# A linear recurrence and its feed-forward block: feed-forward and exclusive decay sum in whole 128x128 tiles, and a new fixed order of steps

## The chip, the cores and the metric

One core of a Trainium2 chip runs the whole kernel. Its engines work in parallel and meet at semaphores: TensorE (matrix products and transposes, results in PSUM), VectorE, ScalarE, GpSimd, and SyncE, which issues most DMAs. The metric is the device time of one execution in microseconds (us); less is better. In the profile's rows PE is TensorE's matrix products, PEld its loads of the stationary operand, DVE is VectorE, ACT ScalarE, POOL GpSimd, SP SyncE.

## The reference

Batch 4, 8 heads, 768 time steps, head size 40; float32 in and out. First a recurrence over time, with a 40x40 state for each of the 32 pairs of batch and head:

```python
for t in range(S):
    y[:, :, t] = np.einsum('bhd,bhde->bhe', rt, state)
    Sa = np.einsum('bhde,bhe->bhd', state, at)
    state_decay = state * wt[:, :, None, :] - np.einsum('bhd,bhe->bhde', Sa, bt)
    state = state_decay + np.einsum('bhd,bhe->bhde', vt, kt)
```

Then y, as 3072 tokens of 320 features (8 heads times 40), goes through a feed-forward block of width 2048:

```python
h = x @ w_in
r = np.maximum(h, 0.0)
g = r * r
return g @ w_out
```

## The kernel before

**Tiling.** Time is cut into 12 chunks of 64 steps (`NCH`, `L`). Within a chunk the recurrence becomes matrix products: cumulative sums of log-decays, scaled copies of k, b, a, r, masked 64x64 triangles, and a state that passes from chunk to chunk. Since a head has 40 features and a chunk 64 steps, nearly all products use half of TensorE's 128x128 array: either two halves of its rows (`64*128` in the rows of the profile: 64 rows, 128 columns) or two halves of its columns (`128*64`). Two such products, one for each half, run at the same time. The kernel calls the two forms "R" and "C" in the third argument of `pe`.

**Steps.** `load`, `prep`, `rec`, `read` and `ffn` make one set of named steps for each chunk; `weights` makes those that load the two matrices. Those that matter here:

- `ld..`: loads of w, k, b, a, v, r, by SyncE (lines 372 to 398), into two buffers each.
- `ln`, `hi`, `lo` (lines 409 to 417): logarithm of the decay, split into two bfloat16 parts.
- `ci`, `cx`, `cg` (lines 430 to 456): inclusive, exclusive and whole sums of the log-decay. `cx` has 8 products of 320 columns, in column halves, against the triangle `UTX` (a 64x64 triangle in each of two diagonal corners of a 128x128 matrix that is zero elsewhere).
- `TK`, `TA`, `TV`, `TS`, `XT`: transposes. `EN`, `CX`: the triangles. `AS`, `EV`, `NU`, `S`, `SC`, `RS`, `Y`: products of the recurrence. Each has a step in small letters that moves its result out of PSUM (`tK`, `mEN`, `u0`, `s` and so on).
- `y` (line 702): VectorE multiplies the result of `Y` by a decay factor and writes it to `Yb`; `yd` (line 708) copies the 640 values once more beside it, so that both halves of the array find them; `XT` (line 721) transposes them in 20 pieces; `xt` moves 1280 columns out of PSUM.
- `F` (line 742): for each chunk four groups u0 to u3 of 20 products of 256 columns, in row halves: 320 features are five blocks of 64, and the two row halves hold the same features of x and different columns of `w_in`. `f`: maximum with zero, by ScalarE or VectorE. `q`: square, by GpSimd or VectorE.
- `O` (line 769): four groups of 16 products of 320 columns, in column halves. `o` moves the result, `st` stores it.

**Order.** Nothing is scheduled by a compiler. The string `ORDER` lists all steps in the order of issue, each with its engine; for TensorE's steps the digit is one of four PSUM slots (`pb0` to `pb3`). Every engine runs its steps strictly in this order, and waits where an operand is not there or a buffer is still in use. Durations that the program gives to `plan.add` (`LAT`, `SWITCH`, `FETCH`, the 2000 of a load) served to make this string and do nothing on the chip. All matrix products are recorded with line 356, all transposes with line 360, since helpers `mm` and `tp` emit them.

Of the kernel before, what the change touches and what calls it, by code (L numbers as in the profile page):

```python
# [7 lines left out]
FP32 = mybir.dt.float32  # L8
BF16 = mybir.dt.bfloat16
# [14 lines left out]
class Plan:  # L24
# [6 lines left out]
    LINE, FETCH = 256, 3500  # L31
# [51 lines left out]
ORDER = """SP ldw 0; SP ldk 0; SP ldw 1; SP ldr 0; ACT ln 0; POOL hi 0; SP ldb 0; POOL zu 2; DVE lo 0; SP lda  # L83
0; PE0 ci 0 h0; PE1 ci 0 h1; POOL zu 1; ACT ei 0 h0; PE2 cx 0; PE cg 0; SP ldr 1; ACT ex 0; ACT ei
0 h1; SP ldw 2; ACT ln 1; ACT eg 0; POOL hi 1; SP ldv 0; DVE mulKB 0 h1; POOL castR 0; DVE mulKB 0
h0; POOL lo 1; PE3 TK 0; SP lda 1; DVE mulA 0; ACT tK 0; POOL zu 0; PE0 ci 1 h0; PE1 TA 0; SP ldk
1; PE2 cx 1; ACT tR 0 g1; DVE tA 0; POOL castR 1; ACT ei 1 h0; DVE tR 0 g0; PE3 EN 0 g1; PE cg 1;
ACT ln 2; DVE mEN 0 g1; SP ldb 1; PE0 EN 0 g0; PE1 ci 1 h1; ACT ex 1; POOL hi 2; DVE mEN 0 g0; ACT
eg 1; ACT castV 0; POOL lo 2; SP ldb 2; ACT ei 1 h1; PE3 EV 0; DVE mulA 1; ACT u0 0 g1; PE2 cx 2;
SP ldv 1; ACT u0 0 g0; PE0 TA 1; ACT tR 1 g1; PE NU 0; PE cg 2; ACT u1 0 g1; DVE u1 0 g0; SP lda  # L90
2; ACT ex 2; DVE tA 1; PE1 S 0; ACT eg 2; POOL mulKB 1 h1; PE3 ci 2 h1; DVE mulKB 1 h0; ACT tR 1
g0; PE2 ci 2 h0; DVE s 0 q0; SP ldk 2; POOL win3; ACT ei 2 h1; PE0 TK 1; DVE s 0 q1; PE3 TV 0; DVE
tK 1; SP ldr 2; ACT tV 0; PE1 EN 1 g0; PE0 EN 1 g1; DVE mEN 1 g0; POOL castV 1; ACT ei 2 h0; PE3
AS 1; DVE mEN 1 g1; PE1 TS 0; PE2 CX 0 g1; ACT tS 0; POOL win1; DVE mCX 0 g1; PE EV 1; SP ldv 2;
PE0 CX 0 g0; ACT u0 1 g1; DVE mCX 0 g0; ACT u0 1 g0; POOL mulKB 2 h1; PE NU 1; DVE mulKB 2 h0; PE1
Y 0; ACT u1 1 g0; PE2 TK 2; DVE y 0; ACT u1 1 g1; SP ldw 3; DVE mulA 2; ACT tK 2; PE0 TV 1; POOL
castR 2; PE1 S 1; DVE yd 0; POOL win0; PE SC 1; DVE tV 1; SP lda 3; PE3 XT 0; PE2 TA 2; ACT xt 0;
DVE s 1 q1; PE0 CX 1 g0; ACT tR 2 g1; DVE s 1 q0; PE3 F 0 u3; ACT tA 2; DVE mCX 1 g0; PE1 TS 1;
POOL castV 2; ACT tR 2 g0; DVE tS 1; PE0 CX 1 g1; ACT f 0 u3; PE2 F 0 u1; SP ldw 4; DVE mCX 1 g1;
ACT ln 3; PE1 EN 2 g0; PE3 EN 2 g1; ACT f 0 u1; POOL hi 3; DVE mEN 2 g0; PE0 RS 1; PE Y 1; SP ldb  # L100
3; POOL lo 3; PE2 AS 2; DVE mEN 2 g1; PE1 F 0 u0; DVE y 1; POOL win2; SP ldk 3; PE EV 2; ACT f 0
u0; PE3 cx 3; DVE yd 1; DVE u0 2 g1; PE0 ci 3 h1; ACT u0 2 g0; PE cg 3; POOL q 0 u1; ACT ei 3 h1;
PE NU 2; ACT eg 3; PE1 ci 3 h0; DVE u1 2 g0; ACT u1 2 g1; PE0 XT 1; ACT ln 4; DVE xt 1; PE2 S 2;
POOL q 0 u0; PE SC 2; ACT ei 3 h0; SP ldr 3; PE0 TV 2; DVE s 2 q0; ACT ex 3; PE1 F 1 u1; DVE tV 2;
POOL wout0; PE3 F 1 u3; ACT f 1 u1; DVE s 2 q1; PE0 F 1 u0; POOL hi 4; ACT f 1 u3; DVE mulA 3;
POOL wout1; PE1 F 0 u2; DVE lo 4; ACT f 1 u0; DVE mulKB 3 h0; PE2 CX 2 g0; POOL mulKB 3 h1; PE3 CX
2 g1; ACT f 0 u2; PE0 F 1 u2; DVE mCX 2 g1; PE1 cx 4; ACT f 1 u2; POOL castR 3; DVE mCX 2 g0; PE
cg 4; POOL wout2; SP ldr 5; PE3 TK 3; ACT ex 4; PE0 ci 4 h0; POOL q 0 u2; DVE tK 3; PE2 TA 3; ACT
eg 4; PE1 RS 2; ACT tR 3 g0; PE Y 2; DVE tA 3; SP ldv 3; ACT tR 3 g1; PE3 O 0 u0; POOL wout3; ACT
ei 4 h0; DVE y 2; SP ldw 5; PE2 EN 3 g0; DVE yd 2; PE O 0 u1; DVE mEN 3 g0; PE0 EN 3 g1; POOL q 1  # L110
u0; PE1 ci 4 h1; DVE mEN 3 g1; PE2 XT 2; ACT ei 4 h1; PE O 0 u2; DVE q 1 u1; POOL q 0 u3; PE1 AS
3; PE0 O 1 u0; SP ldk 4; DVE zu 3; ACT castV 3; DVE q 1 u2; PE O 1 u1; DVE q 1 u3; ACT xt 2; SP
ldb 4; PE EV 3; PE O 1 u2; DVE u0 3 g1; ACT u0 3 g0; PE O 0 u3; PE NU 3; DVE o 0; ACT ln 5; PE O 1
u3; ACT u1 3 g1; DVE u1 3 g0; POOL hi 5; SP st 0; PE2 TS 2; SP lda 4; ACT o 1; POOL zu 4; DVE lo
5; PE3 TV 3; ACT tS 2; PE1 F 2 u1; SP ldr 4; DVE tV 3; POOL castR 5; PE0 F 2 u0; ACT f 2 u1; DVE
mulKB 4 h0; PE2 CX 3 g0; SP ldk 5; PE3 F 2 u3; ACT f 2 u0; POOL q 2 u1; DVE mCX 3 g0; SP lda 5;
PE1 CX 3 g1; PE0 ci 5 h0; ACT f 2 u3; DVE mulKB 4 h1; PE2 F 2 u2; POOL q 2 u0; DVE mCX 3 g1; ACT
ei 5 h0; SP ldb 5; PE3 cx 5; ACT f 2 u2; PE0 RS 3; DVE q 2 u3; PE cg 5; POOL castR 4; PE Y 3; ACT
ex 5; DVE mulA 4; PE1 ci 5 h1; POOL q 2 u2; SP ldv 4; PE2 TK 4; ACT eg 5; DVE y 3; ACT ei 5 h1;
PE3 TA 4; PE1 S 3; DVE tK 4; ACT tA 4; PE SC 3; POOL yd 3; SP ldw 6; PE0 O 2 u0; ACT tR 4 g0; DVE  # L120
s 3 q0; POOL mulA 5; ACT tR 4 g1; PE2 EN 4 g1; PE O 2 u1; DVE mEN 4 g1; SP ldr 6; PE3 XT 3; DVE s
3 q1; POOL mulKB 5 h0; PE2 EN 4 g0; ACT xt 3; PE O 2 u2; DVE mulKB 5 h1; SP st 1; DVE mEN 4 g0;
# [719 lines left out]
```

## Time and profile before

| | us |
|---|---|
| median of 3 runs | 269.33 |
| lowest and highest | 268.33, 271.39 |
| the profiled execution | 270.12 |
| its span, first to last instruction | 268.4 |

The span leaves out what lies around the program, so it is a little less than the time of the same execution. TensorE's granted clock was 0.975 of full speed on average; it was at half speed from 46.7 to 53.5, from 63.8 to 67.2 and from 128.6 to 132.1 us.

| stage of the recurrence or the block, by the groups of the profile | busy us, mean ns of one |
|---|---|
| F, 960 products in row halves | 60.8, 273 |
| O, 768 products in column halves | 59.4, 300 |
| q on GpSimd, 30 | 57.6, 1929 |
| q on VectorE, 18 | 17.5, 979 |
| f on ScalarE, 48 | 49.0, 1024 |

A product's own duration contains its way through the array; products that follow one another overlap, so what one costs is the distance between starts, not its duration. "Idle before" and "waits" say how long an engine stood still and what released it; "issue" there means that the profile names no releaser.

DMA engines were 62.8% busy with SyncE's queue, in packets under 512 bytes for the most part, and nearly all loads are done by 201 us: 165 GB/s in the slice of the span before, 8 GB/s in the one after.

### The profile page before, as it was taken

What the parts mean: (1) busy time and instruction counts of PE and PEld (TensorE: products, weight loads), DVE (VectorE), ACT (ScalarE), POOL (GpSimd) and SP (SyncE); (2) the same over time, 40 slices, a digit from 0 to 9 for tenths busy, and PEclk for the clock granted to TensorE, in tenths of its full rate; (3) what the DMA queues carried; (4) which work ended last, traced back from release to release, by engine and by line L of the source; (5) the groups of instructions that cost most, each with busy time, mean ns of one, the idle gap of its engine ahead of it and who ended that gap; (6) DMA issues with size and microseconds to landing.
All of it is one profiled execution on the core that took longest, in us unless ns stands there. A gap on an engine that the chain in (4) does not pass through costs nothing.

```text
span 268.4 us, 14323 instructions
## 1 busy us (share of the span) xinstructions
PE 226.9 (85%) x6712; PEld 193.6 (72%) x6712; DVE 198.1 (74%) x219; ACT 160.1 (60%) x201; POOL 141.5 (53%) x119
## 2 busy tenths in 40 slices
PE   0557884987979998997998898997879999999992
PEld 0335774776869986876888786886767888878881
DVE  7456578495886797996789898894888697867620
ACT  3346565636735774674674784775756877674631
POOL 4384634086570686674599287793483293232020
PEclk9999999597999999999799999999999999999999
DMA  7999999975993579799898298799980410200213
GB/s 116 185 185 143 153 193 149 136 127 58 171 171 56 114 142 142 180 169 153 181 155 116 53 145 155 133 124 171 158 165 8 89 19 2 54 5 2 51 26 74
DMA packets 135995, 31.06 MB, mean 116 GB/s; under 512 B 125185, under 2 KB 135937, under 8 KB 135937
## 3 DMA queue, kind: packets, MB, share of 16 engines
q1 hardware_dynamic: 131136, 27.53, 62.8%
q0 software_dynamic: 4800, 2.62, 7.7%
q8 instruction: 52, 0.85, 1.4%
q14 instruction: 7, 0.05, 0.1%
HBM read 28.84 MB, written 3.93 MB: 122 GB/s over the span
## 4 chain that ended last, share of the span: by engine, by line
PE 63%; DVE 13%; issue 7%; ACT 5%; DMA 5%; SPq 4%; POOL 3%; ACTq 0%; POOLq 0%; DVEq 0%
PE pb L356 55%; PE pb L360 8%; DMA raw_kb<-in_k_dram 2%; DVE KB L352 2%; DMA raw_r<-in_r_dram 2%; POOL lo L350 1%; ACT VU L342 1%; DVE EN L542 1%; DVE Yb L337 1%; DVE VU L339 1%; SPq L385 1%; SPq L778 1%; POOL tR L346 1%; DVE Yb L702 1%; ACT VUT L342 1%
## 5 line engine op out<-in xcount | busy, mean ns | idle before, releaser
L755 POOL TENSOR_TENSOR G<-G 128x1024 bf16<-128x1024 bf16 x30 | 57.6, 1929 | 53.0 <-ACT G L747 52.6
L356 PE MATMUL pb<-WOUT,G 128*64 128x320 bf16 x768 | 59.4, 300 | 3.8 <-issue 3.7
L747 ACT ACTIVATE G<-pb 128x1024 bf16<-128x1024 f32 x48 | 49.0, 1024 | 22.2 <-PE pb L356 21.1
L356 PE MATMUL pb<-XT,WIN 64*128 64x256 bf16 x960 | 60.8, 273 | 1.0 <-issue 0.9
L356 PEld LDWEIGHTS <-WIN 64*128 64x128 bf16 x960 | 46.9, 96 | 6.4 <-issue 1.7
L356 PEld LDWEIGHTS <-G 128*64 128x64 bf16 x768 | 42.9, 110 | 11.4 <-issue 5.5
L542 DVE TENSOR_TENSOR EN<-pb,MSK 128x1024 bf16<-128x1024 f32 x24 | 29.1, 1221 | 6.3 <-PE pb L356 6.0
L542 DVE TENSOR_TENSOR CX<-pb,MSK 128x1024 bf16<-128x1024 f32 x24 | 29.0, 1218 | 4.4 <-PE pb L356 4.2
L346 POOL CAST hi<-lnW 128x640 bf16<-128x640 f32 x11 | 8.6, 779 | 37.1 <-ACT lnW L409 17.9
L431 ACT ACTIVATE iG<-pb 128x640 f32<-128x640 f32 x24 | 16.8, 702 | 11.3 <-PE pb L356 10.6
L352 DVE TENSOR_TENSOR KB<-raw_kb,iG 128x640 bf16<-128x640 f32 x17 | 18.8, 1113 | 6.2 <-ACT iG L431 3.7
L356 PEld LDWEIGHTS <-EN 128*64 128x64 bf16 x768 | 16.4, 118 | 7.4 <-issue 5.3
L342 ACT ACTIVATE NZ<-pb 64x640 bf16<-64x640 f32 x19 | 13.2, 697 | 13.6 <-PE pb L356 9.0
L634 DVE TENSOR_TENSOR STb<-pb,gL 64x640 bf16<-64x640 f32 x22 | 18.1, 821 | 4.2 <-PE pb L356 3.7
L342 ACT ACTIVATE AR<-pb 128x512 bf16<-128x512 bf16 (+1 forms) x24 | 15.5, 667 | 8.3 <-PE pb L360 5.4
L753 DVE TENSOR_TENSOR G<-G 128x1024 bf16<-128x1024 bf16 x18 | 17.5, 979 | 3.0 <-ACT G L747 3.0
L342 ACT ACTIVATE VU<-pb 64x640 bf16<-64x640 f32 x15 | 10.5, 698 | 9.8 <-PE pb L356 7.3
L339 DVE TENSOR_SCALAR VU<-pb 64x640 bf16<-64x640 f32 x9 | 7.4, 823 | 10.0 <-ACT VU L342 6.2
L350 POOL TENSOR_TENSOR KB<-raw_kb,iG 128x640 bf16<-128x640 f32 x7 | 11.4, 1628 | 5.8 <-DMA raw_kb<-in_k_dram 3.6
L356 PE MATMUL pb<-hi,UTI 64*128 64x320 bf16 x48 | 8.6, 342 | 7.0 <-POOL hi L346 6.9
L342 ACT ACTIVATE osb<-pb 128x640 f32<-128x640 f32 x11 | 7.8, 705 | 11.2 <-PE pb L356 11.1
L350 POOL TENSOR_TENSOR lo<-lnW,hi 128x640 bf16<-128x640 f32 x8 | 13.0, 1622 | 2.4 <-PE pb L360 2.0
(88 smaller groups left out, 454.3 us busy)
## 6 DMA issues: line engine op xcount, KB each, us to landing
raw_w<-in_w_dram SPq DMA_DIRECT2D x24, 160.0 KB, 5.0
raw_kb<-in_k_dram SPq DMA_DIRECT2D x12, 320.0 KB, 6.1
raw_r<-in_r_dram SPq DMA_DIRECT2D x24, 160.0 KB, 4.1
raw_kb<-in_b_dram SPq DMA_DIRECT2D x12, 320.0 KB, 6.7
raw_a<-in_a_dram SPq DMA_DIRECT2D x24, 160.0 KB, 5.2
raw_v<-in_v_dram SPq DMA_DIRECT2D x12, 320.0 KB, 6.6
out_dram<-osb SPq DMA_DIRECT2D x24, 160.0 KB, 2.7
WIN<-in_moe_w_in_dram POOLq DMA_DIRECT2D x8, 160.0 KB, 4.6
```

The costliest lines, as they stand in the source:

```text
L342: alts.append(("ACT", c_act(n), lambda: nc.scalar.activation(out=o_(), in_=i_(), func=ACTF.Copy, scale=1.0 if scale is None else scale)))
L346: lambda: nc.gpsimd.tensor_copy(out=o_(), in_=i_())))
L350: return [("POOL", 130 + 2.35 * n, lambda: nc.gpsimd.tensor_tensor(out=o_(), in0=a_(), in1=b_(), op=op)), ("DVE", c_dve(n), lambda: nc.vec ...
L352: ("DVE", c_dve(n), lambda: nc.vector.tensor_tensor(out=o_(), in0=a_(), in1=b_(), op=op))]
L356: return lambda: nc.tensor.matmul(out=o_(), lhsT=l_(), rhs=r_(), start=start, stop=stop, skip_group_check=True)
L360: return lambda: nc.tensor.transpose(out=o_(), in_=i_(), identity=IDb[rows(g), :])
L431: ew(f"ei {c} h{jh}", [("ACT", c_act(2 * n), lambda hb=hb, jh=jh: nc.scalar.activation(out=iG[0][:].rearrange("p (g j) e -> p g (j e)", g= ...
L542: evac(f"m{nm} {c} g{g}", lambda s, n: [("DVE", c_dve(n), lambda: nc.vector.tensor_tensor(out=dst[q2][:, g, s].rearrange("p q i t -> p (q ...
L634: ew(f"s {c} q{q}", [("DVE", c_dve(2 * n), lambda q=q: nc.vector.tensor_tensor(out=STb[q2][rows(q), :, q, 0:D], in0=slot(hs, FP32)[rows(q) ...
L747: ("ACT", c_act(1024), lambda gb=gb, hf=hf: nc.scalar.activation(out=gb, in_=slot(hf, FP32)[:], func=ACTF.Relu)),
L753: ("DVE", 165 + 0.7 * 1024, lambda gv=gv: nc.vector.tensor_tensor(out=gv, in0=gv, in1=gv, op=ALU.mult)),
L755: ("POOL", 1900, lambda gv=gv: nc.gpsimd.tensor_tensor(out=gv, in0=gv, in1=gv, op=ALU.mult))],
```

## The change

Five edits, and a new `ORDER`. In the third argument of `pe` a form "D" is added for products that use the whole array.

1. `F` has 8 products with 128 rows and 128 columns of the array (two blocks of 128 features, for four groups of 128 columns of `w_in`) instead of 20 halves. A new step `FL` adds the last 64 features in 4 row halves. `f` now follows `FL`. PSUM slot and size of the result are as before.
2. `O` has 8 whole products instead of 16 halves.
3. `cx` has 4 whole products instead of 8 halves.
4. `Yb` holds 320 features and then the last 64 once more; `yd` writes these 64 by the same multiplication from PSUM (128 values in a partition) instead of copying 640; it runs on VectorE only. `XT` has 12 transposes instead of 20, and `xt` moves 768 columns instead of 1280.
5. `WIN` holds 256 features in two blocks of 128, by four DMAs; `WLAST` the last 64 by two DMAs in a new step `wlast`. They were eight DMAs.

In `pe` the durations that served to make the order are restated, and in `load` those of the loads. TensorE's matrix products and transposes go from 6712 to 5800 in all. In the order, `f` is on ScalarE 45 times and on VectorE 3 (48 and 0 before), `q` on GpSimd 37 times and on VectorE 11 (30 and 18); many other moves out of PSUM change between VectorE and ScalarE.

```diff
-    def pe(name, mode, cols, mms, tiles=2, **kw):
+    def pe(name, mode, cols, mms, **kw):
...
-        for jh in range(2):
-            for x in (h_, l_):
-                for g in range(2):
-                    ms.append(mm(
-                        lambda g=g, jh=jh: slot(hx, FP32)[rows(g), jh, 0:n].rearrange(
-                            "p (j e) -> p j e", e=D),
-                        lambda g=g: UTX[:, rows(g)],
...
-        pe(f"cx {c}", "C", n, ms, reads=[("hi",), ("lo",)], writes=[hx], alloc=[hx])
+        for x in (h_, l_):
+            for jh in range(2):
+                ms.append(mm(
+                    lambda jh=jh: slot(hx, FP32)[:, jh, 0:n].rearrange("p (j e) -> p j e", e=D),
+                    lambda: UTX[:],
...
+        pe(f"cx {c}", "D", n, ms, reads=[("hi",), ("lo",)], writes=[hx], alloc=[hx])
...
-        ew(f"yd {c}", copy_alts(lambda: Yb[q2][:, :, :, 1, :], lambda: Yb[q2][:, :, :, 0, :], 640,
-                               True, engines=("DVE", "POOL")),
-           reads=[("Yb", q2, 0)], writes=[("Yb", q2, 1)])
+        def out_y(f0, f1, to):
+            return [("DVE", c_dve(2 * (f1 - f0)), lambda: nc.vector.tensor_tensor(
+                out=Yb[q2][:, :, to:to + f1 - f0], in0=slot(hy, FP32)[:, :, f0:f1],
+                in1=Gex[c % NG][:].rearrange("p (s j) e -> p s (j e)", s=2)[:, :, f0:f1],
+                op=ALU.mult))]
...
+        ew(f"yd {c}", out_y(n - 64, n, n), reads=[hy, ("Gex", c % NG)], writes=[("Yb", q2, 1)],
+           free=[hy])
...
-        for kb_ in range(NKB):
+        for k3 in range(3):
...
-            for i in range(2):
-                for kb_ in range(NKB):
-                    for rg in range(2):
...
-                            lambda rg=rg, kb_=kb_, i=i, u=u: WIN[
-                                rows(rg), kb_, 256 * u + 128 * i:256 * u + 128 * i + 128],
-                            lambda rg=rg, kb_=kb_: XT[q2][rows(rg), kb_, :],
...
-            pe(f"F {c} u{u}", "R", NT, ms, reads=[("XT", q2), ("WIN", u)], writes=[hf],
+            for rg in range(2):
+                for i in range(2):
+                    for k2 in range(2):
...
+                            lambda rg=rg, k2=k2, i=i, u=u: WIN[
+                                :, k2, 512 * u + 256 * rg + 128 * i:
+                                512 * u + 256 * rg + 128 * i + 128],
+                            lambda k2=k2: XT[q2][:, k2, :], i == 0 and k2 == 0, False))
+            pe(f"F {c} u{u}", "D", NT, ms, reads=[("XT", q2), ("WIN", u)], writes=[hf],
                alloc=[hf])
+            ms = []
+            for i in range(2):
+                for rg in range(2):
+                    ms.append(mm(
+                        lambda rg=rg, i=i, hf=hf: slot(hf, FP32)[:, rg, NT * i:NT * i + NT],
+                        lambda rg=rg, i=i, u=u: WLAST[
+                            rows(rg), u, 128 * i:128 * i + 128],
+                        lambda rg=rg: XT[q2][rows(rg), 2, :], False, True))
+            pe(f"FL {c} u{u}", "R", NT, ms, reads=[("XT", q2), ("WLAST",)], writes=[hf])
...
-                    for bb in range(2):
-                        ms.append(mm(
-                            lambda g=g, bb=bb: slot(ho, FP32)[rows(bb), g, 0:DM],
-                            lambda g=g, bb=bb, j=j: G[q2][
-                                :, j, (2 * g + bb) * L:(2 * g + bb) * L + L],
-                            lambda j=j: WOUT[:, j, :], j == 0, j == NFB - 1))
+                    ms.append(mm(
+                        lambda g=g: slot(ho, FP32)[:, g, 0:DM],
+                        lambda g=g, j=j: G[q2][:, j, 2 * g * L:2 * g * L + 2 * L],
+                        lambda j=j: WOUT[:, j, :], j == 0, j == NFB - 1))
```

The beginning of the order, before and after (the whole string has 911 steps before and 960 after):

```diff
-ORDER = """SP ldw 0; SP ldk 0; SP ldw 1; SP ldr 0; ACT ln 0; POOL hi 0; SP ldb 0; POOL zu 2; DVE lo 0; SP lda
-0; PE0 ci 0 h0; PE1 ci 0 h1; POOL zu 1; ACT ei 0 h0; PE2 cx 0; PE cg 0; SP ldr 1; ACT ex 0; ACT ei
+ORDER = """SP ldw 1; SP ldw 0; SP ldr 0; SP lda 0; SP ldb 0; ACT ln 0; SP ldk 0; POOL hi 0; POOL castR 0; DVE
+lo 0; ACT ln 1; PE0 ci 0 h0; SP ldr 2; PE1 cx 0; PE2 ci 0 h1; PE cg 0; ACT ei 0 h1; POOL hi 1; ACT
```

A later place of the new order, where `F` and its `FL` have other steps between them:

```diff
+DVE q 1 u2; PE3 cx 4; ACT o 0; DVE f 2 u3; PE1 F 2 u0; PE2 F 2 u1; SP ldr 4; PE FL 2 u0; POOL
+castV 3; PE0 TS 2; ACT f 2 u0; PE FL 2 u1; DVE tS 2; PE cg 4; PE1 AS 3; ACT ex 4; POOL q 1 u3; SP
```

On TensorE, 808 products and transposes stand ahead of the first `F` in the order before, 952 in the new one.

## The prediction

> **What bounds the kernel now.** I read the page first (busy shares, chain of waits, DMA queues), then TensorE's waits, its timeline, and the windows by stage.
>
> ```profile
> PE 226.9 (85%) x6712; PEld 193.6 (72%) x6712; DVE 198.1 (74%) x219; ACT 160.1 (60%) x201; POOL 141.5 (53%) x119
> PE 63%; DVE 13%; issue 7%; ACT 5%; DMA 5%; SPq 4%; POOL 3%; ACTq 0%; POOLq 0%; DVEq 0%
> q8 instruction: 52, 0.85, 1.4%
> ```
>
> TensorE is the bound, and it executes nearly all of the program: 6712 matmuls and 6712 weight loads of 14323 instructions. The chain has 7% "issue", time in which TensorE waited for nothing that the profile names. The last line offers a cause: 0.85 MB of instructions in 52 packets is 16 KB a packet, and 13424 TensorE instructions over 52 is 258 a packet.
>
> ```profile
> PE pb L356 <- issue: 11.4, 11, 2.9
> PE pb L360 <- issue: 1.3, 2, 0.7
> ```
>
> Thirteen unnamed waits, 12.7 us. The timeline shows where they fall:
>
> ```profile
> 186.95 0.41 PE L360 MATMUL pb<-IDb,Yb 64*128 64x64 bf16 x15 [0.51 <-issue]
> 187.17 0.65 PE L360 MATMUL pb<-IDb,STb 64*128 64x64 bf16 x32
> 187.64 0.65 PE L360 MATMUL pb<-IDb,VU 64*128 64x64 bf16 x32
> 188.27 2.36 PE L356 MATMUL pb<-XT,WIN 64*128 64x256 bf16 x40
> 190.45 0.30 PE L360 MATMUL pb<-IDb,tA 64*128 64x64 bf16 x9
> 191.50 0.29 PE L360 MATMUL pb<-IDb,tA 64*128 64x64 bf16 x7 [0.75 <-issue]
> ...
> 196.32 0.62 PE L356 MATMUL pb<-VU,KB 128*64 128x40 bf16 x27 [0.76 <-issue]
> ...
> 200.60 0.61 PE L356 MATMUL pb<-XT,WIN 64*128 64x256 bf16 x8 [0.90 <-issue]
> ```
>
> From wait to wait there are 15+32+32+40+9 = 128 matmuls, with their weight loads 256 instructions: one packet. Counted over the run, all thirteen waits stand multiples of 128 matmuls apart (once 127, in the middle of operations as here). So TensorE waits for its own code. With loads running, a block of 256 took (200.60-182.40)/4 = 4.55 us where it stalled (182.40 is the wait before these); after the loads end, blocks ran in as little as 3.4 us.
>
> ```profile
> 40.00:66.00 26.00, 19.28 (x629) 16.26 (x628) 18.09 (x19) 15.43 (x20) 12.62 (x13) 0.83 0.83 122
> 66.00:100.00 34.00, 32.39 (x942) 28.78 (x938) 28.44 (x31) 21.25 (x27) 19.01 (x15) 0.98 0.80 126
> 200.60:268.40 67.80, 62.19 (x1755) 52.52 (x1755) 43.24 (x47) 39.69 (x47) 20.68 (x14) 1.00 0.16 34
> ```
>
> Columns: window, length, busy TensorE, weight loads, VectorE, ScalarE, GpSimd, clock, DMA share. Up to 66 us the kernel is filling its pipeline (TensorE 42.9 of 66 us busy); from there on TensorE hardly idles except for code.
>
> **Prices.** `188.27` to `190.45` is 40 feed-forward matmuls in 2.18 us: 54.5 ns each, 109 ns a pair of row halves. In the matmul records the two halves of a pair start 3 ns apart and the next pair 106 ns later here, 132 ns later for the 320 columns of an output matmul: 135 a pair. And changing between row halves and column halves costs:
>
> ```profile
> 78.84 0.41 PE L356 MATMUL pb<-AR,KBT 64*128 64x64 bf16 x16
> 79.18 1.28 PE L356 MATMUL pb<-WOUT,G 128*64 128x320 bf16 x16
> 80.39 0.41 PE L356 MATMUL pb<-AR,KBT 64*128 64x64 bf16 x16
> 80.63 0.30 PE L356 MATMUL pb<-hi,UTI 64*128 64x320 bf16 x2
> ```
>
> The same 16 matmuls take 0.34 us to the next start when column halves follow and 0.24 when row halves do: 0.10 a switch; over all undisturbed switches 90 to 100 ns, I take 95.
>
> **The change, part by part.**
>
> F, FL, O, cx: no row shows a whole tile. A pair costs 109 ns for 256 columns; one whole tile streams the same 256 columns, so F+FL is 8x109 + 2x109 = 1090 ns where F was 10x109 = 1090. O is 8x135 for 8x135, cx 4 for 4. Streaming gain: nothing. The whole tile's weight load could add: at most a whole load's mean, 110 ns (row LDWEIGHTS <-G), at least nothing. I take nothing: in the records a pair's two loads start while the pair before it streams through the same rows, and 109 ns for 256 columns and 135 for 320 are the same 0.42 ns a column, so nothing of a load is left over.
>
> The Trainium skill, page "TensorE: Matmul & The Clock Gate", section "Part 3: Packing small matmuls", says that a weight load overlaps running matmuls only when their row groups differ; in whole tiles they never do. The pair rows above speak against it (same rows, 109 ns). By that rule the sum would be that of the fourth case below.
>
> Switches: counted along TensorE's steps, the order had 97 (row/column). The new one, with whole tiles as a third form, has 188: 53 row/column, 100 whole/row, 35 whole/column. Bounds for one with a whole tile: 0 to 95 ns; I take 95, the only switch seen. 91 x 95 ns = +8.6 us on the bound engine (bounds: 53-97 = -4.2, and +8.6).
>
> XT: 12 transposes for 20, 4 pairs of 29 ns less, 12 times: -1.4 us.
>
> yd and xt:
>
> ```profile
> L702 DVE TENSOR_TENSOR Yb<-pb,Gex 128x640 bf16<-128x640 f32 x12 | 9.8, 817 | 5.1 <-PE pb L356 5.1
> L337 DVE COPY Yb<-Yb 128x640 bf16<-128x640 bf16 x8 | 9.5, 1192 | 0.2
> L337 DVE COPY XT<-pb 128x1280 bf16<-128x1280 bf16 x9 | 7.4, 823 | 4.9 <-PE pb L360 4.8
> ```
>
> yd becomes a multiply of 128 instead of a copy of 640: between 160 ns (817/640 a column, no fixed part) and 817; I take 0.3 us. It lies between Y and XT, but TensorE waited on Yb only twice, 1.3 us. xt moves 768 for 1280. Together -1.5 us (0 to -3). All other engine moves, counts times mean durations: VectorE about -8 us, ScalarE -7, GpSimd +11 (37 squares of 1.93 us instead of 30). None is the bound; I count nothing.
>
> A new wait: f now waits for FL, which can come several steps after F (F 6 u3 and FL 6 u3 have O, RS, NU, Y, O between: 1.08+0.29+0.50+0.50+1.08 us by their rows). ScalarE's later steps and the PSUM slot (one of four) wait with it. Zero while the other slots feed TensorE, up to 3.5 us where not; I take 0.
>
> Code: 5800 matmuls make 45.3 blocks instead of 52.4, and fewer short ones. I added up each block's steps from the prices above. Before, the 29 blocks from 68.5 to 200.6 us need 112.5 us of TensorE; blocks under 4.55 us are short by 22.8 us in all; measured, the stretch lost 132.1-112.5 = 19.6, 86% of that. In the new order the blocks from the tenth to the last load are short by 9.4; times 0.86, 8.1. Gain 11.6 us. The blocks are longer because each has more whole matmuls and more switches: part of the 8.6 us above is spent where TensorE would have stood still.
>
> Start: raw_w 1 is now issued before raw_w 0, 1.46 us of SyncE; `ln 0` began at 5.24 us, and `lo 0` waited until 7.87 for VectorE's clearing, so about 1 us of that is hidden, +0.5 remains. castR 0 no longer stands behind lo 1 on GpSimd, which released TA 0 at 18.16: -1 to -2 us. Against that 952 instead of 808 matmuls stand before the first F; at 4.55 us per 128 that is up to +5.1. SyncE's loads move by a few places (ldr 2 ahead of ldv 0, ldv 2 ahead of lda 3); one that waits for its buffer holds those behind it, with a chunk's lead as before. The weights' issues are on GpSimd, six for w_in instead of eight, ahead of the first F as before. Net 0, bounds -2 and +5.
>
> Sum: 8.6 - 1.4 - 1.5 - 11.6 = -5.9 us on the span of 268.4: 262.5. The profiled execution took 270.12, the median is 269.33, 0.9 above the span: 263.4.
>
> **Rivals.**
> 1. Sum holds: 263.4; own range 259 to 268.
> 2. A whole tile needs no drain: 135 switches x 95 ns = 12.8 us less, of which 4.2 goes back (0.28 us a block, in the 15 load-stage blocks under 4.55 us): 255. For: no row shows such a switch. Against: every change of form seen costs 95.
> 3. The start eats it: +5.1, 268.5. For: TensorE is slow up to 66 us, and the new order puts 18% more small matmuls there.
> 4. Whole loads are not hidden: 816 x 29 ns (the smallest pair step of the trace) = +24, 287, up to 816 x 110. Against: the pair rows.
> 5. Code fetch gives nothing back, slower: stretches of small matmuls, which stall, hardly change, and each block is refused until its packet lands, however few there are; the switches stay, 268.4+8.6-1.4 (XT) +0.9 = 276.5. It decides if the unnamed waits fall by less than 7.2 us of 12.7.
>
> The Trainium skill, page "Runtime: NRT & Kernel Launch", section "Instruction fetch mechanics", has the 256-instruction blocks but calls their cost mostly hidden, so that fewer instructions gain nothing: case 5. The 13 waits disagree.
>
> **Numbers.** Chances: 0.42, 0.15, 0.18, 0.05, 0.20 in this order. 1% (266.6 to 272.0) is about what a measurement can tell. Faster: 0.38 + 0.15 + 0.04 = 0.57; within: 0.04 + 0.12 + 0.02 = 0.18; slower: 0.02 + 0.05 + 0.18 = 0.25. Range 254 to 277: it takes in 2, 3 and 5 and leaves out 4 and half of the edges.
>
> **What would show it.** Right: unnamed waits under 6 us, still 128 matmuls apart; F's eight at 109 ns; +95 ns from F to FL; TensorE's span 66 us to the end no worse. Wrong: whole tiles further apart than 109 and 135 ns; first F after 55 us; unnamed waits above 6 us.

## The result, and the profile after

The kernel became slower: 288.14 us (median of 4 runs, 286.29 to 288.9) against 268.83 us for the kernel before (4 runs, 267.15 to 271.39); ratio 1.073, 95% interval 1.065 to 1.082. A ratio, here and below, is taken over the executions within 1.5% of the fastest of the same kernel, so it is not always the quotient of the printed medians. Forecast were 263.4 us, with a range of 254 to 277. The span grew from 268.4 to 284.6 us, 16.2 us more. The granted clock does not explain it: two executions of the changed kernel at 0.974 and 0.920 of full speed have spans of 286.7 and 286.1 us.

The page of the changed kernel, its span, busy shares, chain of waits and the instruction queue:

```profile
span 284.6 us, 12538 instructions
PE 238.1 (84%) x5800; PEld 180.7 (63%) x5800; DVE 198.9 (70%) x224; ACT 152.0 (53%) x196; POOL 150.9 (53%) x117
PE 51%; DVE 16%; DMA 8%; ACT 7%; SPq 7%; issue 6%; POOL 2%; POOLq 1%; DVEq 0%; ACTq 0%
q8 instruction: 45, 0.74, 1.2%
```

The instructions shrank as forecast (45 packets for 52), but TensorE carries 51% of the chain of waits instead of 63%: DVE, DMA, SyncE's queue and ACT have taken the rest. The forecast's third line, windows by stage (columns as before):

```profile
40.00:66.00 26.00, 22.16 (x590) 17.77 (x584) 15.56 (x18) 14.16 (x19) 6.16 (x7) 1.00 0.80 123
66.00:100.00 34.00, 29.63 (x585) 21.30 (x584) 25.48 (x27) 15.21 (x20) 17.93 (x14) 0.95 0.87 122
200.60:284.60 84.00, 73.71 (x1678) 56.02 (x1670) 48.56 (x53) 44.82 (x52) 46.75 (x27) 0.98 0.28 53
```

At 200.6 us 1678 of 5800 matmuls are still to come, and the rest of the run takes 84 us where it took 67.8. TensorE's waits, what it waited for, sum, times and longest:

```profile
PE pb L363 <- POOL hi L353: 10.1, 2, 9.2
PE pb L363 <- DVE Sb L344: 5.0, 1, 5.0
PE pb L363 <- DVE NZ L346: 3.7, 5, 1.6
PE pb L363 <- DVE VU L346: 2.2, 3, 1.0
PE pb L367 <- DVE Yb L707: 2.1, 1, 2.1
PE pb L363 <- issue: 1.8, 2, 1.2
```

The 12.7 us of unnamed waits are 1.8. In their place stand waits for named steps. The first row is mostly the wait for the first matmul (9.2 us; 6.9 before); behind the start the longest is a single one of 5 us.

**A ledger.** I took the distance from each matmul's start to the next one's, and subtracted the step's own price from undisturbed rows and 95 ns for a switch. What is left over falls into waits of a step's first matmul, delays inside a step (half clock among them), and waits 128 matmuls apart (code). What counts as a wait for a step and what as a delay inside one depends on how the line is drawn; their sum does not:

```
us                         before   after   difference
prices and switches         202.1   209.3      +7.2
ahead of the first matmul     6.9     9.2      +2.3
waits for a step to begin    27.4    42.7     +15.3
delays inside a step         10.4    15.5      +5.1
code                         16.2     2.5     -13.7
sum                                           +16.2
```

The first and the last line are what the prediction worked out. The middle three are what it set at about nothing.

**The largest wait, followed back.** The timeline of the changed kernel around it (start, length, what; in brackets the idle time before it and its releaser):

```profile
126.89 1.25 POOL L353 CAST VU<-raw_v 64x1280 bf16<-64x1280 f32 x1 [6.21 <-DMA raw_v<-in_v_dram]
128.02 6.23 DVE L767 TENSOR_TENSOR G<-G 128x1024 bf16<-128x1024 bf16 x1
128.11 5.58 POOL L769 TENSOR_TENSOR G<-G 128x1024 bf16<-128x1024 bf16 x3
134.17 0.81 DVE L344 COPY Sb<-pb 128x1280 bf16<-128x1280 bf16 x1
134.30 0.10 PEld L363 LDWEIGHTS <-G 128*128 128x128 bf16 x1 [4.39 <-DVE G L767]
135.03 1.23 PE L363 MATMUL pb<-WOUT,G 128*128 128x320 bf16 x4 [5.02 <-DVE Sb L344]
```

Read from below: `O 3 u0` waits 5.02 us, for two things that stand one behind the other on VectorE: its operand, the square `q 3 u0`, which its weight load waits for until 134.30, and `tS 3` (the copy to Sb), which frees its PSUM slot. VectorE stood 6.23 us in that one square, which takes 0.68 to 0.69 us where nothing runs beside it. Beside it GpSimd does three squares without a break, 128.11 to 133.69, and VectorE ends 0.56 us behind the last. GpSimd's squares come in a row because it was late: it waited 6.21 us for `raw_v`. SyncE's timeline says why that load came late:

```profile
50.62 1.33 SPq L382 DMA_DIRECT2D raw_w<-in_w_dram  x2
78.58 1.20 SPq L403 DMA_DIRECT2D raw_r<-in_r_dram  x2
109.86 12.22 SPq L790 DMA_DIRECT2D out_dram<-osb  x4
122.13 0.62 SPq L396 DMA_DIRECT2D raw_v<-in_v_dram  x1
```

`ldv 5` stands behind the stores `st 1` and `st 2`, and `st 2` waits for `o 2`, which ended at 120.8 us. The first two rows show another such stand: `ldr 5`, with all later loads behind it, waits 23.5 us for `castR 3` to free its buffer (10.9 us at the same place before), and between 57 and 71 us the DMA engines move 44 and 6 GB/s.

The squares in the groups of the profile, VectorE's and GpSimd's:

```profile
L767 DVE TENSOR_TENSOR G<-G 128x1024 bf16<-128x1024 bf16 x11 | 18.9, 1715 | 0.4 <-ACT G L761 0.4
L769 POOL TENSOR_TENSOR G<-G 128x1024 bf16<-128x1024 bf16 x37 | 71.4, 1939 | 53.4 <-ACT G L761 52.7
```

Eleven squares on VectorE take more than eighteen did before (17.5 us, 979 ns each). Four of the eleven take over 1 us: 3.49 us at 73.8, 2.44 at 89.9, 6.23 at 128.0 and 1.60 at 200.1. The wait at 135 us is not the only one behind such a square:

```profile
73.75 3.49 DVE L767 TENSOR_TENSOR G<-G 128x1024 bf16<-128x1024 bf16 x1
79.82 0.35 PE L367 MATMUL pb<-IDb,Yb 64*128 64x64 bf16 x12 [2.10 <-DVE Yb L707]
89.86 2.44 DVE L767 TENSOR_TENSOR G<-G 128x1024 bf16<-128x1024 bf16 x1
93.49 0.64 PE L367 MATMUL pb<-IDb,STb 64*128 64x64 bf16 x32 [0.46 <-DVE G L763]
```

Between the first two rows VectorE runs `mulKB`, `y`, `mulKB` and `yd` without a break, and `XT 2` waits for the last; between the other two it runs `f 2 u3`, which frees the PSUM slot of `TS 2`. The three waits are 7.6 us together, of 16.2 that the span grew.

### The profile page after: what moved, and what is told of

Read it like the earlier page. It is cut to its first block, busy times and chain, and to the rows that moved or that the text cites. A ratio compares the mean times of both kernels' runs of the same rounds, so it can differ in the third digit from the quotient of the medians.

```text
span 284.6 us, 12538 instructions
## 1 busy us (share of the span) xinstructions
PE 238.1 (84%) x5800; PEld 180.7 (63%) x5800; DVE 198.9 (70%) x224; ACT 152.0 (53%) x196; POOL 150.9 (53%) x117
## 4 chain that ended last, share of the span: by engine, by line
PE 51%; DVE 16%; DMA 8%; ACT 7%; SPq 7%; issue 6%; POOL 2%; POOLq 1%; DVEq 0%; ACTq 0%
PE pb L363 44%; PE pb L367 7%; DMA raw_a<-in_a_dram 6%; SPq L403 3%; DVE G L767 2%; DVE NZ L346 2%; DMA raw_kb<-in_b_dram 2%; DVE STb L638 2%; POOL G L769 2%; DVE KB L359 2%; DVE VU L346 2%; ACT VU L349 2%; ACT NZ L349 1%; ACT AR L349 1%; SPq L382 1%
## 5 line engine op out<-in xcount | busy, mean ns | idle before, releaser
L769 POOL TENSOR_TENSOR G<-G 128x1024 bf16<-128x1024 bf16 x37 | 71.4, 1939 | 53.4 <-ACT G L761 52.7
L363 PE MATMUL pb<-WOUT,G 128*128 128x320 bf16 x384 | 60.5, 305 | 6.7 <-DVE Sb L344 5.0
L761 ACT ACTIVATE G<-pb 128x1024 bf16<-128x1024 f32 x45 | 45.2, 1023 | 35.4 <-PE pb L363 35.3
L363 PE MATMUL pb<-XT,WIN 128*128 128x256 bf16 x384 | 50.4, 279 | 2.6 <-DVE CX L546 1.0
L363 PEld LDWEIGHTS <-G 128*128 128x128 bf16 x384 | 35.4, 99 | 23.2 <-DVE G L767 4.8
L363 PEld LDWEIGHTS <-WIN 128*128 128x128 bf16 x384 | 36.0, 99 | 11.0 <-issue 4.5
L546 DVE TENSOR_TENSOR EN<-pb,MSK 128x1024 bf16<-128x1024 f32 x24 | 29.0, 1219 | 8.3 <-PE pb L363 8.1
L546 DVE TENSOR_TENSOR CX<-pb,MSK 128x1024 bf16<-128x1024 f32 x24 | 29.0, 1219 | 6.9 <-PE pb L363 6.6
L357 POOL TENSOR_TENSOR KB<-raw_kb,iG 128x640 bf16<-128x640 f32 x10 | 16.3, 1628 | 21.8 <-ACT iG L438 12.5
L363 PE MATMUL pb<-XT,WLAST 64*128 64x256 bf16 x192 | 18.0, 278 | 0.0
L707 DVE TENSOR_TENSOR Yb<-pb,Gex 128x640 bf16<-128x640 f32 (+1 forms) x24 | 12.5, 552 | 7.8 <-PE pb L363 7.6
L353 POOL CAST hi<-lnW 128x640 bf16<-128x640 f32 x6 | 4.3, 719 | 21.9 <-ACT lnW L416 13.2
```

Source lines behind the costliest of these rows:

```text
L357: return [("POOL", 130 + 2.35 * n, lambda: nc.gpsimd.tensor_tensor(out=o_(), in0=a_(), in1=b_(), op=op)), ("DVE", c_dve(n), lambda: nc.vec ...
L363: return lambda: nc.tensor.matmul(out=o_(), lhsT=l_(), rhs=r_(), start=start, stop=stop, skip_group_check=True)
L546: evac(f"m{nm} {c} g{g}", lambda s, n: [("DVE", c_dve(n), lambda: nc.vector.tensor_tensor(out=dst[q2][:, g, s].rearrange("p q i t -> p (q ...
L707: return [("DVE", c_dve(2 * (f1 - f0)), lambda: nc.vector.tensor_tensor(out=Yb[q2][:, :, to:to + f1 - f0], in0=slot(hy, FP32)[:, :, f0:f1] ...
L761: ("ACT", c_act(1024), lambda gb=gb, hf=hf: nc.scalar.activation(out=gb, in_=slot(hf, FP32)[:], func=ACTF.Relu)),
L769: ("POOL", 1900, lambda gv=gv: nc.gpsimd.tensor_tensor(out=gv, in0=gv, in1=gv, op=ALU.mult))],
```

## The experiments

Ratios are to the kernel before on the same chip, with 95% intervals; a point is 1% of the time of the kernel before; the change itself is at 1.073.

**Which half of the change.** The whole tiles with the order of before, and the half-array products with the new order. First edit, against the kernel before, in `ORDER` (and edits 1 to 5 as in the change):

```diff
-PE3 F 0 u3; ACT tA 2
+PE3 F 0 u3; PE FL 0 u3; ACT tA 2
...
-DVE y 0; ACT u1 1 g1
+DVE y 0; DVE yd 0; ACT u1 1 g1
...
-POOL win3; ACT ei 2 h1
+POOL win3; POOL wlast; ACT ei 2 h1
```

> The changed kernel's whole tiles in the order of before: FL right behind its F, yd right behind its y. It has 236 changes of form on TensorE (97 before, 188 in the changed kernel) and needs 213.9 us of TensorE by the step prices (202.1 before, 209.3 changed). Theory A (the order loses the time: its waits, not the tiles): +11.8 us of TensorE, -10.7 us of code waits, so about 270 us (267 to 274), well below the changed kernel. Theory B (the tiles lose it in any order, by FL behind F, longer-held PSUM slots, switches): at least as slow as the changed kernel, 284 us or more.

Measured: 269.03 us against 272.52, 0.988 [0.982, 0.995]. TensorE's waits have these two unnamed rows:

```profile
PE pb L360 <- issue: 4.6, 4, 1.5
PE pb L364 <- issue: 2.1, 2, 1.6
```

The code waits halve with the old order too, in spite of 236 switches. Second edit, against the changed kernel: the products as before, and in the new order

```diff
-DVE y 1; PE FL 0 u0; PE2 TV 2
+DVE y 1; DVE yd 1; PE2 TV 2
...
-PE3 F 0 u3; DVE s 2 q0; PE FL 0 u3; PE FL 1 u0; DVE s 2 q1
+PE3 F 0 u3; DVE s 2 q0; DVE s 2 q1
...
-DVE s 1 q0; POOL wlast; PE1 TK 2
+DVE s 1 q0; PE1 TK 2
```

> The half-array kernel of before in the new order (FL and wlast left out, yd right behind its y on VectorE). TensorE needs 204.9 us. Theory A (the order loses the time): as slow as the changed kernel or slower, since the code waits come back: 281 to 292 us. Theory B (the tiles lose it): near before, 262 to 274 us.

Measured: 290.48 us against 272.52, 1.060 [1.040, 1.080]. So the tiles by themselves gain 1.2%, and the order by itself loses 6%. It is the order. The two do not simply add up: the whole change loses 7.3%, more than the 4.8% of the sum, and what the tiles cost in the new order was not measured closely enough (1.040 to 1.080) to say why.

**O alone.** The kernel before with only edit 2:

```diff
-                    for bb in range(2):
-                        ms.append(mm(
-                            lambda g=g, bb=bb: slot(ho, FP32)[rows(bb), g, 0:DM],
...
+                    ms.append(mm(
+                        lambda g=g: slot(ho, FP32)[:, g, 0:DM],
```

> Before, with O alone in whole tiles, in the order of before. 132 changes of form instead of 97 (+3.3 us of TensorE), 384 matmuls fewer, so 3 blocks of code fewer; the blocks between 68 and 200 us are short by 17.2 us instead of 22.8 (-4.8 us). Theory A: 267 us, between 265 and 270. Theory B (whole tiles cost more than their switches): 272 us or more.

Measured: 271.45 us, 0.999 [0.993, 1.006]. The 35 more switches (132 for 97) are 3.3 us at 95 ns each; TensorE's unnamed waits in this run are 11.2 us, only 1.5 fewer than before, where the expectation has 4.8. What made up for the rest is not shown.

**SyncE's stands.** First the load at 52 us:

```diff
-DVE tK 3; SP ldr 5; PE0 F 2 u3
+DVE tK 3; SP ldr 4; PE0 F 2 u3
...
-PE2 F 2 u1; SP ldr 4; PE FL 2 u0
+PE2 F 2 u1; SP ldr 5; PE FL 2 u0
```

> The changed kernel with two of SyncE's loads exchanged, ldr 4 for ldr 5, so that the 23.5 us in which SyncE stands at ldr 5 (until castR 3 has freed the buffer) and no load starts go. If this stand delays later chunks (theory A1): 3 to 6 us faster than the changed kernel, 282 to 285 us. If other things are late by then anyway (theory A2): no change, 287 to 289 us.

Measured: 287.44 us against 272.52, 1.059 [1.046, 1.071]; the interval overlaps the change's own. Then that swap and, in SyncE's own sequence, the stores `st 1` and `st 2` behind later loads:

```diff
-SP ldr 6; SP st 1; SP st 2; SP ldv 5; SP ldw 7; SP lda 6; SP ldk 6
+SP ldr 6; SP ldv 5; SP ldw 7; SP st 1; SP lda 6; SP st 2; SP ldk 6
```

> The changed kernel with SyncE's queue mended in two places: ldr 5 behind ldr 4 and others, and st 1, st 2 behind the loads ldv 5, ldw 7, lda 6 that they held up for 12.2 us. All other engines keep their steps. Theory C (late loads make GpSimd run its squares in a bunch, which shuts VectorE out; one square took 6.23 us at 128 us and TensorE then waited 5.1 us): 4 to 7 us faster than the changed kernel, 281 to 284 us. Theory D (many small waits on chains of steps, spread over the order): 286 to 288 us.

Measured: 282.25 us against 270.96, 1.045 [1.035, 1.055].

**VectorE's stretched squares.** Four go to ScalarE, as an activation:

```diff
+                ("ACT", 1100, lambda gv=gv: nc.scalar.activation(
+                    out=gv, in_=gv, func=ACTF.Square)),
...
-DVE q 0 u0
+ACT q 0 u0
...
-DVE q 1 u2
+ACT q 1 u2
...
-DVE q 3 u0
+ACT q 3 u0
...
-DVE q 6 u3
+ACT q 6 u3
```

> The changed kernel with the four squares of VectorE that GpSimd stretched (3.49, 2.44, 6.23 and 1.60 us instead of 0.69) on ScalarE, in the same places of the order. Theory C: VectorE gets 13.8 us back in the places where TensorE waits, 5 to 9 us faster, 279 to 283 us. Theory D: 286 to 288 us.

Measured: 278.34 us against 270.96, 1.031 [1.021, 1.040]. The group of VectorE's remaining squares:

```profile
L764 DVE TENSOR_TENSOR G<-G 128x1024 bf16<-128x1024 bf16 x7 | 4.8, 686 | 0.4 <-ACT G L758 0.4
```

All seven now take their time alone, and the wait of 5 us for Sb is gone from TensorE's list, as it is in the run before this one. Not all of the stretch is gone: at 73.87 us it passed to the next VectorE instruction with two operands in SBUF, a `mulKB` that took 3.62 us (0.81 in the changed kernel), and `XT 2` still waits 0.83 us. Both mends in one kernel:

> The changed kernel with both mends, SyncE's queue and the four squares on ScalarE. Alone they gave 0.974 and 0.960 of the changed kernel's ratio to before (1.045 and 1.031 against 1.073). Theory C with two separate losses: 1.005 to 1.02 of before. If both mend the same wait at 128 us: as with the squares alone, 1.025 to 1.035.

Measured: 278.29 us against 272.29, 1.024 [1.016, 1.033]. 2.8 and 4.3 points singly, 4.9 together: each removes the same wait behind the square at 128 us.

**Are stretched squares bad by themselves?** The same move in the order of before, with whole tiles (six squares) and with the kernel before (seven):

```diff
-PE0 RS 3; DVE q 2 u3; PE cg 5
+PE0 RS 3; ACT q 2 u3; PE cg 5
...
-SP ldb 11; DVE q 6 u3; PE2 TA 9
+SP ldb 11; ACT q 6 u3; PE2 TA 9
```

> Whole tiles in the order of before, and six squares of VectorE that GpSimd stretched (0.85 to 2.17 us instead of 0.69, 4.1 us too much in all) on ScalarE. In this order TensorE waited only 4.5 us for other engines' steps after 140 us. If VectorE's lateness still costs something here: 0.975 to 0.985 of before. If not: 0.985 to 0.99, as without.

> Before, with its seven stretched squares (1.20 to 1.67 us) on ScalarE, nothing else. Theory C says that what counts is a stretched square ahead of a TensorE step that has nothing to fill the gap; before waits for code in the same stretches. 0.99 to 1.0 of before. Under 0.98 would mean that before lost as much by it as the new order, and the comparison of orders would need another cause.

Measured: 270.36 us against 272.29, 0.994 [0.990, 0.999], no better than without the move (0.988); and 272.21 us, 1.001 [0.996, 1.006]. In the order of before the same contention costs nothing that can be seen: in its trace no engine is listed as having waited for one of VectorE's squares. In the changed kernel's waits one row is:

```profile
PEld L363 <- DVE G L767: 4.8, 2, 4.4
```

The price of a stretched square is what stands behind it.

**GpSimd's squares made short.** To take away all that GpSimd's squares do at once, its lateness too, they square 256 of the 1024 columns only; the other 768 stay unsquared, so these kernels leave out a part of the computation and serve for the time alone:

```diff
                 ("POOL", 1900, lambda gv=gv: nc.gpsimd.tensor_tensor(
-                    out=gv, in0=gv, in1=gv, op=ALU.mult))],
+                    out=gv[:, 0:256], in0=gv[:, 0:256], in1=gv[:, 0:256], op=ALU.mult))],
```

in the kernel with both mends, in the whole tiles with the old order, and in the changed kernel:

> The new order with both mends (1.024 of before), and GpSimd squares only the first 256 of the 1024 columns of each of its 37 groups; the other columns stay unsquared. GpSimd does some 54 us less. Theory C (what is left of the new order's loss is VectorE shut out by GpSimd: mulKB took 2.52, 2.32 and 2.14 us instead of 0.82 at 146, 210 and 221 us, TensorE's waits for VectorE follow): 0.98 to 1.0 of before, within 1% of the old order with the same short squares. Theory D (chains of steps with too little beside them, whatever GpSimd does): 1.015 or more, still 2.5% above the old order.

> Whole tiles in the order of before (0.988), with the same short squares on GpSimd (30 groups); the other columns stay unsquared. TensorE is the bound there: 0.975 to 0.985 of before by theory C and theory D alike; it is what the two others are compared with.

> The changed kernel itself with the same short squares on GpSimd (37 groups); the other columns stay unsquared, SyncE's queue is not mended. Theory C: GpSimd late and VectorE shut out are the whole loss but for SyncE's stands: 0.99 to 1.01 of before (the changed kernel: 1.073). Theory D: 1.03 or more.

Measured: 275.06 us, 1.015 [1.010, 1.021]; 267.51 us, 0.987 [0.980, 0.992]; 275.20 us, 1.014 [1.008, 1.019], all against 270.83. The old order has no use for short squares (0.988 with whole ones). The new order gains 6 points by them, and then the two mends bring nothing. The two groups in the changed kernel with short squares:

```profile
L769 POOL TENSOR_TENSOR G<-G 128x256 bf16<-128x256 bf16 x37 | 25.0, 681 | 76.2 <-ACT G L761 72.3 <-DVE G L763 3.6
L767 DVE TENSOR_TENSOR G<-G 128x1024 bf16<-128x1024 bf16 x11 | 9.8, 895 | 0.4 <-ACT G L761 0.4
```

The square at 128 us is now one of 1.28 us at 122.80. So of the 8.5 points between the two orders (1.073 and 0.988), about 6 hang on GpSimd's long squares, and 2.7 (1.014 and 0.987) do not. Short squares shut VectorE out less and make GpSimd early as well, so this run alone does not part the two; moving four squares of VectorE away, with GpSimd's left long, gave 4.3 of the 6.

**Where are the rest?** Four runs with two orders joined, the order of before (as in the first run) up to a point, and behind it the steps that are left in the order of the changed kernel: up to `F 1 u1` (about 66 us) and up to `S 5` (about 140 us), with whole and with short squares. The places of joining, against the old order:

```diff
-ACT ex 3; PE1 F 1 u1; PE FL 1 u1; DVE tV 2; POOL wout0
+ACT ex 3; PE1 F 1 u1; POOL zu 3; PE3 F 0 u2; PE FL 0 u2
...
-ACT f 4 u3; PE3 S 5; DVE mCX 5 g0; PE SC 5; POOL castV 6
+ACT f 4 u3; PE3 S 5; POOL zu 7; DVE mCX 5 g0; POOL q 4 u2
```

> Whole tiles; the steps up to F 1 u1 (about the first 66 us) in the order of before, all others in the new order. Theory S (the new start costs it): most of the difference to the old order goes, 271 to 276 us. By the account of work done (at 60 us the new order is only 1.0 us behind the old order with the same tiles, at 140 us 7.9): 284 to 287 us.

> The same with the steps up to S 5 (about the first 140 us) in the order of before. Theory S: 271 to 276 us. By the account of work done the new order loses half of its time after 140 us: 277 to 282 us. If all is lost between 60 and 140 us: 270 to 274 us.

> Whole tiles, the order of before up to F 1 u1 (about 66 us), the new order behind it, and GpSimd squares only 256 of the 1024 columns of each piece (768 stay unsquared), so that its squares are short. With short squares the new order throughout stands at 1.0135 [1.0084, 1.0187] of the kernel before and the old order throughout at 0.9865 [0.9806, 0.9924]: 2.7 points are left between them. Theory Start (all that is left is lost in the first 66 us, where the new order has fewer steps beside its chains): 0.985 to 0.995. Theory Spread (it is lost along the whole run, where EV, NU and S wait one behind the other): 1.000 to 1.010. Between the two: both.

> The same with the order of before up to S 5 (about 140 us). Theory Start: as with the old order up to 66 us, within half a point. Theory Spread: half of what is left at 66 us is gone, 0.993 to 1.000. If it stays above the run with the old start by a point, the place where the two orders are joined costs time of its own, and neither run can be read as a sum of stages.

Measured, in this order: 283.32 us, 1.042 [1.028, 1.055]; 279.02 us, 1.033 [1.024, 1.042]; 274.07 us, 1.006 [1.001, 1.011]; 278.30 us, 1.025 [1.019, 1.032]. The last one stands 1.9 points above the one before it although more of it is the old order: joining costs time of its own (1.5 us before `cx 7` at 142 us, a wait that neither order has), so these runs can't be added up by stage, as the expectation said. What its ledger does show is that the late waits belong to the late part of the new order: after 140 us 10.8 us of waits for a step to begin, as in the new order throughout (11.0), where the old order has 3.9. The old start alone brings 3 points with whole squares; with short ones 0.7, in intervals that overlap.

The ledgers of the two orders with short squares, from the profiled executions (spans 264.9 and 274.6 us):

```
us                              old order   new order   difference
prices and switches                 213.7       209.2      -4.5
ahead of the first matmul             6.9         9.5      +2.6
waits for a step, up to 60 us        12.8        17.5      +4.7
   60 to 140 us                       5.3         5.1      -0.2
   after 140 us                       3.9        11.0      +7.1
delays inside a step                  8.8        12.7      +3.9
code                                  8.0         4.0      -4.0
```

After 140 us the new order waits where a step of the recurrence follows the one that it needs with little between, among them 1.06 us before `S 9`, 1.13 before `F 8 u3`, 0.78 before `NU 10`, 0.69 before `F 9 u3`; these four are in the changed kernel's trace with the same lengths. The old order with short squares has no wait for a step over 0.25 us after 184 us. I filled the four:

```diff
-PE FL 8 u0; PE2 TK 10; PE1 S 9; PE SC 9; PE0 TV 9; PE O 7 u2
+PE FL 8 u0; PE2 TK 10; PE O 7 u2; PE1 S 9; PE SC 9; PE0 TV 9
...
-PE0 F 8 u1; PE3 F 8 u3; PE FL 8 u3; PE FL 8 u1
+PE0 F 8 u1; PE FL 8 u1; PE3 F 8 u3; PE FL 8 u3
...
-PE3 TA 11; PE NU 10; PE1 O 8 u0; PE2 F 9 u3
+PE3 TA 11; PE1 O 8 u0; PE NU 10; PE O 8 u1; PE2 F 9 u3
```

> The changed kernel with GpSimd squaring only 256 of the 1024 columns of each piece (768 stay unsquared), and four feed-forward steps moved on TensorE: O 7 u2 ahead of S 9, FL 8 u1 ahead of F 8 u3, O 8 u0 ahead of NU 10, O 8 u1 ahead of F 9 u3. In the run without the moves (1.0135 [1.0084, 1.0187]) TensorE waits there 1.06 us before S 9, 1.13 before F 8 u3, 0.78 before NU 10 and 0.69 before F 9 u3, 3.65 us in all, and in the order of before, with the same short squares, for none of the last chunks' steps over 0.25. Theory Chains (what the new order still costs is lost where a chain's next step follows with too little between): about 3 us less, 0.999 to 1.005, and none of the four waits above 0.4 us. Theory Latency (the chain itself, not TensorE, ends the run there, so that the waits only move to the steps behind): 1.010 to 1.017, with as much waiting after 205 us as without the moves.

Measured: 275.9 us against 271.0, 1.023 [1.014, 1.031], no faster than without the moves. In TensorE's timeline of this run the matmuls that waited in that stretch:

```profile
213.99 0.31 PE L360 MATMUL pb<-hi,UTI 64*128 64x320 bf16 x2 [0.38 <-ACT VUT L346]
220.48 1.03 PE L360 MATMUL pb<-XT,WIN 128*128 128x256 bf16 x8 [0.65 <-DVE CX L543]
225.31 1.25 PE L360 MATMUL pb<-WOUT,G 128*128 128x320 bf16 x8 [0.56 <-DVE XT L341]
228.88 1.91 PE L360 MATMUL pb<-XT,WIN 128*128 128x256 bf16 x16 [0.53 <-DVE VU L343]
232.29 0.41 PE L360 MATMUL pb<-AR,KBT 64*128 64x64 bf16 x16 [0.49 <-ACT G L758]
```

`S 9` and `NU 10` no longer wait. `F 8 u3` and `F 9 u3` (second and fourth row) still do, 0.65 and 0.53 us, and `ci 11`, `O 8 u0` and `EN 11` wait where they did not: the waits moved, and filling a few gaps by hand is not enough.

**A version with fewer switches.** Whole tiles in the old order, with six squares on ScalarE, `cx` in column halves again and `FL` behind the next `F` where two follow (205 switches instead of 236):

```diff
-PE1 F 1 u1; PE FL 1 u1; DVE tV 2; POOL wout0; PE3 F 1 u3; PE FL 1 u3
+PE1 F 1 u1; DVE tV 2; POOL wout0; PE3 F 1 u3; PE FL 1 u1; PE FL 1 u3
```

> The kernel with squares on ScalarE, old order and whole tiles, but cx in column halves again and FL behind the next F where two F follow one another: 205 changes of form instead of 236, 48 matmuls more. At 95 ns a change 2.9 us less of TensorE. If a change of form costs what the rows say: 1.1% under the kernel without this edit, about 0.965 to 0.975 of before. If changes of form hide behind waits: no difference.

Measured: 269.83 us against 272.29, 0.997 [0.992, 1.002], against 0.994 with the switches. Taking 31 switches away showed no gain. TensorE's waits have two rows that the run with the switches has not:

```profile
PE pb L360 <- ACT G L761: 2.0, 4, 0.7
PE pb L364 <- ACT G L761: 0.6, 1, 0.6
```

These are waits for `f` on ScalarE to free its PSUM slot, and `f` follows `FL`: moving `FL` behind the next `F` cost 2.6 us where the switches saved 2.9. So this run does not tell what a switch costs. The version with the lowest ratio among those that compute everything stays the first run, whole tiles in the order of before, 0.988 [0.982, 0.995]; the intervals of its two variants overlap with its own.

## Why the prediction was wrong

**Right: the price of whole tiles.** Timeline of the changed kernel, a stretch without waits:

```profile
222.88 1.26 PE L363 MATMUL pb<-WOUT,G 128*128 128x320 bf16 x8
223.98 1.04 PE L363 MATMUL pb<-XT,WIN 128*128 128x256 bf16 x8
224.95 0.39 PE L363 MATMUL pb<-XT,WLAST 64*128 64x256 bf16 x4
225.18 0.40 PE L363 MATMUL pb<-AR,KBT 64*128 64x64 bf16 x16
```

From `F` to `FL` 0.97 us: eight at 109 ns and a switch of 95 make 0.967. Over all undisturbed pairs of starts, the median of a whole tile is 109 ns for 256 columns and 136 for 320; forecast were 109 and 135. The fourth rival falls; that its 287 us lies near the measured 288.1 is an accident. With it falls, for this case, the rule of the Trainium skill, page "TensorE: Matmul & The Clock Gate", section "Part 3: Packing small matmuls", that a weight load overlaps running matmuls only when their row groups differ: here they are the same rows each time and nothing of a load is left over.

**Right: a switch to or from a whole tile costs a switch.** Whole to rows 205 ns to the next start where 109 is the price, 232 where it is 136: 96 each. Rows to whole 122 for 26, columns to whole 118 for 28. The second rival falls. Prices and switches together grew by the 7.2 us that the working has (8.6 less 1.4).

**Right in direction, a little small: code.** The unnamed waits fell from 12.7 to 1.8 us; by the ledger, code gave back 13.7 us where 11.6 were forecast. The fifth rival falls by its own condition. With the same tiles in the old order 6.7 us of unnamed waits are left, so a part of the 10.9 less comes with the new order and not with the fewer instructions, presumably because its other waits cover them.

**Wrong: "None is the bound; I count nothing."** This is the step that failed, with the neighbouring "a chunk's lead as before" for SyncE's loads: the term for the other engines stood at nothing, and TensorE's waits and delays grew by 22.7 us (15.3, 5.1 and 2.3 in the ledger). I multiplied counts by mean durations and had VectorE about 8 us shorter, ScalarE 7 shorter and GpSimd 11 longer. ScalarE (160.1, then 152.0 us) and GpSimd (141.5, then 150.9) did so; VectorE did not get shorter at all (198.1, then 198.9). GpSimd's added squares also made others longer, and a mean of 979 ns hid that a square of VectorE takes 0.68 us alone and, in the trace of before, 1.2 to 1.67 beside an instruction of GpSimd. That was to be had from the records of before, by asking for the shortest, middle and longest square, here before and after:

```profile
L753 DVE TENSOR_TENSOR G<-G x18: 679/692/1666, 82.0 to 256.6; 128x1024 bf16<-128x1024 bf16 x18
L767 DVE TENSOR_TENSOR G<-G x11: 679/693/6228, 73.8 to 275.6; 128x1024 bf16<-128x1024 bf16 x11
```

The price was not the time that VectorE lost but the place: in the order of before no one waits for these squares, in the new one TensorE's next step needs the square itself and the copy behind it. The experiments give 4.3 points of the 8.5 to four stretched squares, and about 6 to GpSimd's long squares with all that they do, its own lateness included. The late loads are a part of the same chain and not a second cause: with short squares the two mends bring nothing (1.015 and 1.014).

The Trainium skill, page "SBUF — State Buffer", section "SBUF: two separate sides", has the mechanism: VectorE, with two operands in SBUF, and GpSimd share a pair of ports, one holds it for a whole instruction, and the other fully blocks. The trace agrees that a square is shut out and not slowed by a share: 6.23 us, ended 0.56 us after GpSimd's third. By that page of the Trainium skill the instruction that starts first gets the pair. Two places agree: at 128.02 us GpSimd was still in its cast (126.89 to 128.14), and at 275.61, where VectorE began 0.10 us ahead, its square took 0.69 us and GpSimd's 2.34 instead of 1.89. A third does not plainly: at 73.75 VectorE began 1.02 us ahead of GpSimd's square and still ended 0.56 us behind it; until 74.76 GpSimd was issuing DMAs. When a waiting instruction is let in is open too: at 128 us VectorE came in neither behind the cast nor between the three squares; in the trace of before, at 195.15 us, it came in between two that stood as close (1.66 us, and GpSimd's second took 2.34).

**Wrong: "Net 0, bounds -2 and +5" for the start.** The first `F` came at 60.8 us (50.1 before), past the 55 that was named as a sign of error; prices and switches worth 19.8 us were done by 60 us, 23.9 before. The loss of 4.1 us lies inside the bounds, at the upper end, so the third rival was part of the answer. Of the order's loss the start is the smaller part; how much it keeps at the end of the run is open, since a joined order costs time of its own.

**The wait of f for FL, "I take 0"; Yb, about 1.3 us.** One wait of TensorE in the changed kernel, 0.46 us before `TS 2`, is for a PSUM slot that `f` holds, and there `f` was late behind a stretched square, not behind `FL`; so that zero stands here. It does not hold in every order: the run with `FL` behind the next `F` has 2.6 us of such waits. Yb cost 2.1 us in one wait, before `XT 2`, and this one too stands behind a stretched square; `yd` takes 283 ns (0.3 us forecast), `y` 820. But the stages from 66 us on, which should have been no worse, took 218.6 us for 202.4.

**What stays open:** 2.7 points between the two orders with short squares. The ledgers put them in waits for a step to begin, 4.7 us up to 60 us and 7.1 after 140; filling four of these did not bring them back. The likeliest reading, argued and not shown, is that the new order runs the recurrence's chain of steps too close to what TensorE needs next over its whole length, so that a gap filled here opens behind.

## What to carry to other kernels

A kernel whose engines follow one written order should be costed by what each wait for a step would be, not by busy sums: here the bound engine's own work and its code came out within 2.1 us of the forecast, and the waits of the new order (15.3, 5.1 and 2.3 us) cost 22.7. Change tiles and order separately, with the old order adapted by the fewest steps: that version has the lowest ratio of those that compute everything, and it shows at once which half loses. Before work is moved to GpSimd, look at single records of VectorE's two-operand SBUF instructions for their shortest and longest time, and at what stands behind the long ones.

## What was not expected of the hardware

- A VectorE square can be shut out through several GpSimd instructions in a row: 0.68 us alone, 2.44 and 3.49 us beside others, 6.23 us beside three back to back. `mEN` and `mCX`, which have one operand in PSUM, are not stretched: 1219 ns on average, 1221 and 1218 before.
- The same contention has no price in one order (1.001 for seven squares taken away) and about 4 points in another (1.073 to 1.031 for four).
- 31 switches of 95 ns less, 2.9 us of TensorE's time, did not show in the time (0.997 and 0.994): the order that saved them brought 2.6 us of waits for `f`.
